# Transposing V and weight tiles in the loading DMA instead of on TensorE, in the backward pass of a two-layer decode kernel

## The chip, the cores and the metric

The kernel runs on one core of one Trainium2 chip. The metric is the device time of one execution, in microseconds. A few runs of the kernel before are repeated in each set, on the same chip as the kernels they are compared with. A ratio is the mean time of one kernel's fast runs over that of the other's of the same rounds, so it is not quite the ratio of the medians that stand beside it; its 95% interval is in brackets.

Engines in the profile: PE is TensorE (PEld its weight loads), DVE is VectorE, ACT is ScalarE, SP is SyncE, which issues the loads. SPq and ACTq are the two queues from which loads are issued here.

## The reference, cut to what matters

Forward and backward of two layers with one new token for each of two sequences. Attention runs over caches of 16384 positions, so each layer streams K and V (4 heads x 2 sequences x 16384 x 128, 32 MiB each), and the weights are used once per pass. The two layers share caches and weights.

```python
q = (x @ wq)...                                    # wq 1024 x 4096
scores = jnp.einsum("bhqd,bhkd->bhqk", q, k) * (Dh ** -0.5)
p = _softmax(scores); o = jnp.einsum("bhqk,bhkd->bhqd", p, v)
x = x + o.reshape(B, Sq, Hq * Dh) @ wo             # wo 4096 x 1024
h = _gelu(jnp.einsum("bsd,df->bsf", y, w1) + b1)   # w1 1024 x 3584
x = x + jnp.einsum("bsf,fd->bsd", h, w2) + b2
# ... two such layers, then jax.vjp: gradients of x, K, V and all weights
```

The backward products need the other orientation of what the forward pass used: dP = dO V^T needs V with its 128 columns on the partitions, and the products with w1, wo and wq of the backward pass need those weights transposed.

## The kernel before

Tiles are 128 partitions x 4096 bf16 (1 MiB; a w1 tile is 128 x 3584), in a pool of 7 load buffers. All loads are issued by SyncE. Where a transposed tile is needed, TensorE turns eight 128x128 blocks at a time into PSUM and VectorE or ScalarE copies them back to SBUF.

```python
def emit_T(cv, b, third):                       # V of the backward attention, K of the forward one
    tp = (px if third and tp_n["n"] % 3 == 0 else pt)([128, 8, 128], BF16, "tp")
    for j in range(8):
        PE.transpose(tp[:, j, :], cv[:, b * 8 + j, :], ident[:])
    kT = ktp.tile([128, 8, 128], BF16, name="kT", tag="kT")
    evac_bf16(kT[:]..., tp[:]..., 1024)         # VectorE or ScalarE, whichever has less to do
    return kT

class BwdPipe:                                  # w1 and wo of the backward products
    def push(self, wv, j, jj, o0, on):
        for o in range(on):
            PE.transpose(tp[:, o, :], wv[:, j, (o0 + o) * 128:(o0 + o + 1) * 128], ident[:])
        ...
    def pop(self):
        for o in range(on):
            PE.matmul(wide_out(self.out_ps, 2 * jj), lhsT=wT[:, o, :], rhs=wide_in(self.gT[:, o0 + o, :]), ...)

class Ahead:                                    # a weight turned in place ahead of its products: w2, wo of layer 0
    def row(self, j): ...; turn(w, ...)
    def products(self, j, out_ps, gT_bf): ...
# ...
# layer-1 backward attention: w2 rows join wq's rows in one list of side work, worked off between slots
                    wq_q.extend(n[2])                         # 8 transposes of wq rows
                if g == groups[-1] and c == 0 and b == 3:
                    for k in range(NLD - 2):
                        ahead.load(k)
                        wq_q.extend(lambda j=j: ahead.row(j) for j in range(j0, j0 + rb))
```

## Time and profile before

1181 us (1177.89 to 1181.94). The part that the change touches lies between the end of the layer-1 forward pass (459.5 us) and the start of the last stage (761.6 us):

| stretch of the kernel before | us |
|---|---|
| w1 and wo backward, layer 1 | 52.6 |
| layer-1 backward attention with wq, and the w2 tail | 190.7 |
| w2 product, then w1 and wo backward, layer 0 | 58.8 |
| last stage (layer-0 backward attention and all gradient stores) | 421.2 |

The page of the kernel before: first busy time per engine, then the span in 40 slices (busy share of the DMA engines in tenths, and what they moved).

```profile
span 1182.8 us, 40678 instructions
PE 981.7 (83%) x17981; PEld 754.3 (64%) x17981; DVE 606.4 (51%) x1264; ACT 538.2 (46%) x1366; POOL 63.9 (5%) x113
DMA  9999999998999989989999939767999999999996
GB/s 370 416 417 417 417 417 395 393 341 365 417 417 413 412 312 416 393 327 414 411 396 383 365 136 398 293 231 296 372 403 420 420 413 418 419 421 418 423 423 267
```

PE at 83% looks like the bound, but the DMA row is full almost everywhere, at 417 GB/s in many slices (423 at most). Averages over the span settle nothing; the stretches do. The windows view of the kernel before, for the four stretches of the table: length, then busy us (and count) of PE, PEld, DVE, ACT, POOL, then the granted TensorE clock, the DMA share and GB/s.

```profile
459.50:512.10 52.60, 43.95 (x965) 42.50 (x965) 28.09 (x74) 17.96 (x32) 0.00 (x0) 0.92 1.03 399
512.10:702.80 190.70, 169.41 (x3589) 144.74 (x3590) 72.56 (x158) 67.08 (x118) 0.00 (x0) 0.95 0.89 349
702.80:761.60 58.80, 51.56 (x1201) 48.50 (x1198) 27.59 (x70) 19.15 (x34) 0.71 (x1) 0.94 0.90 341
761.60:1182.80 421.20, 363.90 (x4749) 217.95 (x4748) 305.33 (x532) 282.62 (x541) 57.86 (x98) 0.75 0.94 380
```

In the first stretch the DMA is full. In the second and third both PE and DMA are at about 90%: two limits that nearly balance. The groups of instructions that the change removes, in the kernel before between 459 and 772 us (count, busy us, mean ns, idle before them):

```profile
L379 PE MATMUL tp<-ident,kv_V 128*128 128x128 bf16 x864 | 69.9, 227 | 7.7 <-DMA kv_V<-in_A_v_cache_dram 6.3 <-issue 0.6 <-DVE kT L151 0.2
L263 PE MATMUL wtp<-ident,wt 128*128 128x128 bf16 x704 | 56.9, 228 | 2.5 <-DMA wt<-in_B_w_dram 1.3 <-issue 1.2
L313 PE MATMUL wtq<-ident,wqt 128*128 128x128 bf16 x256 | 20.3, 224 | 2.0 <-DMA wqt<-in_A_wq_dram 1.8
```

Matmuls are pipelined: a mean of 227 ns is not what one costs. The timeline of PE in the kernel before (start, us, what) gives the true cost. Eight transposes start 0.45 us before the products that follow them, so about 56 ns each; and there is no gap at all.

```profile
745.07 0.61 PE L313 MATMUL turn<-ident,wt 128*128 128x128 bf16 x8
745.52 0.35 PE L340 MATMUL wob_b<-gA_all,wt 128*128 128x32 bf16 x8
745.72 0.61 PE L313 MATMUL turn<-ident,wt 128*128 128x128 bf16 x8
```

Two views of the loads. The DMA part of the page says in how many packets they moved, and how many of these were small; the timeline of SyncE's queue shows that issuing a 1 MiB load takes it 0.33 us.

```profile
DMA packets 89133, 449.35 MB, mean 380 GB/s; under 512 B 7026, under 2 KB 7026, under 8 KB 49788
593.85 0.33 SPq L368 DMA_DIRECT2D kv_V<-in_A_v_cache_dram  x1
594.59 0.33 SPq L368 DMA_DIRECT2D kv_K<-in_A_k_cache_dram  x1
```

### The profile page before, as it was taken

Reading aid. Unit: us, or ns where it says so; the run is one execution under the profiler, and the core shown is the slowest. Engines: PE = TensorE matmul, PEld = TensorE weight load, DVE = VectorE, ACT = ScalarE, POOL = GpSimd, SP = SyncE. Lnnn points to the kernel's source line nnn. Section 1 sums busy time; section 2 is a strip of 40 time slices with the busy share of each in tenths; the row PEclk is TensorE's granted clock in tenths of the full one; section 3 lists DMA queues with packets and bytes.
Section 4 is the critical chain, followed back from the end, with each engine's and each line's share of the span. In section 5 each row is a group of like instructions: output and inputs, shape, how many; then the busy total and the mean of one; then the engine's idle time right before and its main releaser. Section 6 shows DMA issues by size and latency. Waiting matters only on the chain. (4 is left out here: it accounts for less than half of the span.)

```text
span 1182.8 us, 40678 instructions
## 1 busy us (share of the span) xinstructions
PE 981.7 (83%) x17981; PEld 754.3 (64%) x17981; DVE 606.4 (51%) x1264; ACT 538.2 (46%) x1366; POOL 63.9 (5%) x113
## 2 busy tenths in 40 slices
PE   4989795488879876899798988888988889999885
PEld 3867673488767756887676788755555554555552
DVE  1544351233535423444243334567877877786774
ACT  0544341022535421334233323366766867685773
POOL 0000000000000000000000000001111111111111
PEclk9988886597989876989998998987877877786785
DMA  9999999998999989989999939767999999999996
GB/s 370 416 417 417 417 417 395 393 341 365 417 417 413 412 312 416 393 327 414 411 396 383 365 136 398 293 231 296 372 403 420 420 413 418 419 421 418 423 423 267
DMA packets 89133, 449.35 MB, mean 380 GB/s; under 512 B 7026, under 2 KB 7026, under 8 KB 49788
## 3 DMA queue, kind: packets, MB, share of 16 engines
q1 hardware_dynamic: 72204, 348.17, 73.9%
q0 software_dynamic: 16752, 98.59, 20.3%
q8 instruction: 140, 2.29, 0.8%
q14 instruction: 37, 0.30, 0.1%
HBM read 348.14 MB, written 98.58 MB: 378 GB/s over the span
## 5 line engine op out<-in xcount | busy, mean ns | idle before, releaser
L148 ACT COPY kT<-tp 128x512 int32<-128x512 int32 x181 | 106.3, 587 | 266.0 <-PE tp L379 258.2
L151 DVE COPY kT<-tp 128x1024 bf16<-128x1024 bf16 x187 | 128.1, 691 | 152.7 <-PE tp L379 143.1
L379 PE MATMUL tp<-ident,kv_K 128*128 128x128 bf16 x1728 | 144.7, 233 | 4.6 <-DMA kv_K<-in_A_k_cache_dram 4.0
L379 PEld LDWEIGHTS <-kv_K 128*128 128x128 bf16 x1728 | 109.9, 104 | 5.2 <-DMA kv_K<-in_A_k_cache_dram 5.1
L159 DVE CAST big<-xm 128x512 bf16<-128x512 f32 (+1 forms) x140 | 91.0, 685 | 30.3 <-PE xm L1100 15.9
L156 ACT CAST big<-xm 128x512 bf16<-128x512 f32 (+1 forms) x157 | 85.7, 593 | 25.1 <-PE xm L959 15.1
L521 PEld LDWEIGHTS <-kT 128*128 128x128 bf16 x2048 | 76.7, 98 | 28.7 <-issue 22.9
L521 PE MATMUL sc<-qT_bf,kT 128*128 128x8 bf16 x2048 | 92.2, 171 | 0.7 <-issue 0.7
L263 PE MATMUL wtp<-ident,wt 128*128 128x128 bf16 x928 | 77.0, 231 | 3.6 <-issue 2.3
L297 PEld LDWEIGHTS <-wt 128*128 128x128 bf16 x1696 | 49.1, 103 | 46.4 <-issue 15.3
L485 ACT ACTIVATE e_all<-sc,negm 128x64 bf16<-128x64 f32 x256 | 77.1, 343 | 1.3 <-DVE negm L480 1.1
L379 PE MATMUL tp<-ident,kv_V 128*128 128x128 bf16 x864 | 69.9, 227 | 7.7 <-DMA kv_V<-in_A_v_cache_dram 6.3
L159 DVE CAST keepK<-xm 128x512 bf16<-128x512 f32 x95 | 61.7, 684 | 18.8 <-PE xm L1100 13.6
L405 PE MATMUL acc_all<-kv_V,e_all 128*16 128x256 bf16 x864 | 46.5, 295 | 29.2 <-DMA kv_V<-in_A_v_cache_dram 16.2
L148 ACT COPY wT<-wtp 128x512 int32<-128x512 int32 (+1 forms) x60 | 34.5, 576 | 78.2 <-PE wtp L263 63.4
L151 DVE COPY wT<-wtp 128x1024 bf16<-128x1024 bf16 (+1 forms) x64 | 40.5, 636 | 52.0 <-PE wtp L263 48.7
L156 ACT CAST keepK<-xm 128x512 bf16<-128x512 f32 x102 | 54.8, 592 | 19.7 <-PE xm L1100 18.9
L263 PEld LDWEIGHTS <-wt 128*128 128x128 bf16 x928 | 58.9, 103 | 4.4 <-issue 2.9
L379 PEld LDWEIGHTS <-kv_V 128*128 128x128 bf16 x864 | 54.6, 102 | 9.8 <-DMA kv_V<-in_A_v_cache_dram 7.3
L159 DVE CAST keepV<-xm 128x512 bf16<-128x512 f32 (+1 forms) x78 | 50.8, 685 | 18.8 <-PE xm L1100 14.8
L156 ACT CAST keepV<-xm 128x512 bf16<-128x512 f32 (+1 forms) x94 | 51.0, 594 | 19.8 <-PE xm L1100 16.8
L485 ACT ACTIVATION_READ_ACCUMULATOR e_all<-sc,negm 128x1 f32 x256 | 59.8, 234 | 0.0
(325 smaller groups left out, 1762.7 us busy)
## 6 DMA issues: line engine op xcount, KB each, us to landing
kv_K<-in_A_k_cache_dram SPq DMA_DIRECT2D x81, 1024.0 KB, 12.9
kv_V<-in_A_v_cache_dram SPq DMA_DIRECT2D x81, 1024.0 KB, 11.9
out_dram<-big POOLq DMA_DIRECT2D x36, 1024.0 KB, 17.0
wt<-in_A_wo_dram SPq DMA_DIRECT2D x32, 1024.0 KB, 11.1
wt<-in_B_w_dram SPq DMA_DIRECT2D x32, 896.0 KB, 14.4
out_dram<-keepK POOLq DMA_DIRECT2D x22, 1024.0 KB, 17.3
out_dram<-keepV POOLq DMA_DIRECT2D x18, 1024.0 KB, 17.2
wt<-in_A_wq_dram SPq DMA_DIRECT2D x16, 1024.0 KB, 9.1
```

The lines of the kernel that those rows point to most:

```text
L148: S.copy(out=dst.bitcast(I32), in_=src.bitcast(I32))
L151: V.tensor_copy(out=dst, in_=src)
L156: S.copy(out=dst, in_=src)
L159: V.tensor_copy(out=dst, in_=src)
L263: PE.transpose(tp[:, o, :], wv[:, j, (o0 + o) * 128:(o0 + o + 1) * 128], ident[:])
L297: PE.matmul(fps[:, jo, :].rearrange("p (a b) -> p a b", b=2), lhsT=wv[:, j, jo * 128:(jo + 1) * 128], rhs=xT_bf[:, j0 + j, :].unsqueeze(1) ...
L379: PE.transpose(tp[:, j, :], cv[:, b * 8 + j, :], ident[:])
L405: PE.matmul(self.acc[cg:cg + 16, :], lhsT=coef(u), rhs=self.cv[:, t:t + 2, :].rearrange("p t d -> p (t d)"), start=False, stop=True, tile_ ...
L485: S.activation(out=e_all[:, g, f * half:(f + 1) * half, l, h, :], in_=sc[g][f][:, h, :].rearrange("p (a b) -> p a b", b=2), func=ACT.Exp, ...
L521: PE.matmul(sc[g][f][:, :, t % TH], lhsT=kT[:, j, :], rhs=q_bf[:, g, :], start=True, stop=True)
```

## The change

The intent is to take these transposes off TensorE, and their copies off VectorE and ScalarE, by letting the DMA crossbar transpose while it loads. 67 loads become transposing ones: 27 of V, 8 of wq, 16 of wo, 16 of w1, 65 MiB in all (27 + 8 + 16 + 14). K, w2, and everything in the forward pass and the last stage stay as they were, but for one kept V tile (tile XG below), which is turned in place in layer 1 and then used turned in the last stage.

```diff
+    def w_load_T(W, j0, rb, c0, n_cols):
+        wt = ld.tile([128, LDW], BF16, name="wtT", tag="ld")
+        wv = wt[:, 0:rb * n_cols].rearrange("p (o r) -> p o r", r=rb * 128)
+        nc.sync.dma_start_transpose(wv, W[j0 * 128:(j0 + rb) * 128, c0:c0 + n_cols])
+        return wv
+    def products_T(wv, j, jj, out_ps, gT):
+        for o in range(JO):
+            PE.matmul(wide_out(out_ps, 2 * jj), lhsT=wv[:, o, j * 128:(j + 1) * 128], rhs=wide_in(gT[:, o, :]), ...)
+    def v_load_T(g, c):
+        t = ld.tile([128, LDW], BF16, name="kv_VT", tag="ld")
+        tv = t[:].rearrange("p (t d) -> p t d", d=128)
+        nc.sync.dma_start_transpose(tv, Vv[g, :, c * TC:(c + 1) * TC, :].rearrange("p t d -> p (t d)"))
+        return tv
# ... layer-1 backward attention
-                        cv = kv_load("V", g, c)
-                    kTs[s] = emit_T(cv, b, True)
-                    if s % 7 == 3 and v_turns:
+                        cv = held_tiles["V"][:]... if (g, c) == (XG, 0) else v_load_T(g, c)
+                    kTs[s] = cv[:, b * 8:(b + 1) * 8, :]
+                    if s % 5 == 3 and v_turns:
# ... w1 and wo of layer 1 (and, likewise, both of layer 0, where wo had been turned ahead)
-        _, dmps = w_pass(B_w1, D, F, "dm_ps", gT_bf=dh_all[:, :, lsl(l)])
+        dmps = w_bwd(B_w1, D, F, "dm_ps", dh_all[:, :, lsl(l)])
-        _, dops = w_pass(A_wo, HD, D, "do_ps", gT_bf=gA_all[:, :, lsl(l)])
+        dops = w_bwd(A_wo, HD, D, "do_ps", gA_all[:, :, lsl(l)])
# ... wq: loaded transposed; its list of transposing steps is now empty
+                box[j] = w_load_T(A_wq, j, 4, kv * D, D)
+        turns = [lambda j=j: turn_row(j) for j in range(DJ)] if get_ is not None else []
# ...
```

More of the change, by code (lines that the diff above doesn't have):

```diff
@@ L251, in w_load, with w_bwd @@
         return wv
+    def w_load_T(W, j0, rb, c0, n_cols):
[4 more added lines that the diff above has]
+    def products_T(wv, j, jj, out_ps, gT):
+        JO = wv.shape[1]
+        for o in range(JO):
+            PE.matmul(wide_out(out_ps, 2 * jj), lhsT=wv[:, o, j * 128:(j + 1) * 128], rhs=wide_in(gT[:, o, :]),
+                      start=(o == 0), stop=(o == JO - 1))
+    def w_bwd(W, n_in, n_out, name, gT):
+        ps = px([128, 512], F32, name)
+        for j0, rb in w_chunks(n_in, n_out):
+            wv = w_load_T(W, j0, rb, 0, n_out)
+            for j in range(rb):
+                products_T(wv, j, j0 + j, ps, gT)
+        return pairs(ps, n_in // 128)
     class BwdPipe:
@@ L589, in attn_bwd @@
         last_q = []
-        v_turns = deque(lambda c=c, b=b: turn(held_tiles["V%d" % c][:, b * 1024:(b + 1) * 1024],
+        v_turns = deque(lambda w=w, b=b: turn(held_tiles[w][:, b * 1024:(b + 1) * 1024],
                                               lambda: pt([128, 8, 128], BF16, "turn"))
-                        for c in range(NCH) for b in range(NB))
+                        for w in ["V"] + ["V%d" % c for c in range(NCH)] for b in range(NB))
         while s < len(slots) + 2 or sch.busy():
@@ L600, in attn_bwd @@
                     if b == 0:
-                        cv = kv_load("V", g, c)
-                    kTs[s] = emit_T(cv, b, True)
-                    if s % 7 == 3 and v_turns:
+                        cv = held_tiles["V"][:].rearrange("p (t d) -> p t d", d=128) if (g, c) == (XG, 0) else \
+                            v_load_T(g, c)
+                    kTs[s] = cv[:, b * 8:(b + 1) * 8, :]
+                    if s % 5 == 3 and v_turns:
                         v_turns.popleft()()
@@ L779, in load @@
         def load(j):
-            wt = ld.tile([128, LDW], BF16, name="wqt", tag="ld") if get_ is None else get_("wq", kv, j)
-            box[j] = wt[:].rearrange("p (j n) -> p j n", j=4)
             if get_ is None:
-                nc.sync.dma_start(box[j], wq_v[:, j:j + 4, kv * D:(kv + 1) * D])
+                box[j] = w_load_T(A_wq, j, 4, kv * D, D)
+            else:
+                box[j] = get_("wq", kv, j)[:].rearrange("p (j n) -> p j n", j=4)
         def turn_row(j):
@@ L790, in products @@
             for j in range(DJ):
+                if get_ is None:
+                    products_T(box[j - j % 4], j % 4, j, ps, dq_all[:, hs, 2 * l:2 * l + 2])
+                    continue
                 for o in range(8):
@@ L800, in dq_in @@
                 V.tensor_copy(out=dq_all[:, hs, 2 * l + b], in_=dqT[:, b * HKV + kv, :])
-        return [lambda j=j: load(j) for j in (0, 4)], dq_in, [lambda j=j: turn_row(j) for j in range(DJ)], products
+        turns = [lambda j=j: turn_row(j) for j in range(DJ)] if get_ is not None else []
+        return [lambda j=j: load(j) for j in (0, 4)], dq_in, turns, products
     def attn_in_bwd(l, gT, dn, hook=lambda: None):
@@ L851 @@
     sv = saved["m0"]
-    _, dmps = w_pass(B_w1, D, F, "dm_ps", gT_bf=dh_all[:, :, lsl(0)])
-    wob = Ahead(A_wo, HD, "wob")
-    for k in range(len(wob.chunks)):
-        wob.load(k)
-    rest = deque(lambda j=j: wob.row(j) for j in range(wob.J - 4))
+    dmps = w_bwd(B_w1, D, F, "dm_ps", dh_all[:, :, lsl(0)])
     dm = wrk.tile([128, DJ, 2], F32, name="dm_sb")
     V.tensor_copy(out=dm[:], in_=dmps[:])
-    dn = ln_bwd(dm[:], sv["y2"][:], sv["rstd2"][:], "dn", lambda: some(rest, 4))
-    dx = ln_bwd(dn[:], sv["y1"][:], sv["rstd1"][:], "dx", lambda: some(rest, 4))
+    dn = ln_bwd(dm[:], sv["y2"][:], sv["rstd2"][:], "dn")
+    dx = ln_bwd(dn[:], sv["y1"][:], sv["rstd1"][:], "dx")
     g1 = vec.tile([128, DJ, 2], F32, name="gM0")
@@ L863 @@
     V.tensor_copy(out=gA_all[:, :, lsl(0)], in_=g1[:])
-    dops = px([128, 512], F32, "wob_b")
-    for j in range(wob.J + 4):
-        some(rest, 1)
-        if j >= wob.J - 4 and j < wob.J:
-            wob.row(j)
-        if j >= 4:
-            wob.products(j - 4, dops, gA_all[:, :, lsl(0)])
+    dops = w_bwd(A_wo, HD, D, "wob_b", gA_all[:, :, lsl(0)])
     TP = [pt([128, 8, 128], BF16, "tpm%d" % i) for i in range(2)]
@@ L873 @@
         V.memset(t[:].bitcast(F32), 0.0)
-    do_delta(0, pairs(dops, HQ))
+    do_delta(0, dops)
     rowsA = ld.tile([128, LDW], BF16, name="rowsA", tag="ld")
@@ L1175, in score0 @@
             return
+        if (g, c) == (XG, 0):
+            done("V", g, c)
         if c == 0:
@@ L1241 @@
                 cv = get("V", *chunks[i])[:].rearrange("p (t d) -> p t d", d=128)
-                kT = ktp.tile([128, 8, 128], BF16, name="kT", tag="kT")
-                tp = mtp()
-                for j in range(8):
-                    PE.transpose(tp[:, j, :], cv[:, b * 8 + j, :], ident[:])
-                evac_bf16(kT[:].rearrange("p a b -> p (a b)"), tp[:].rearrange("p a b -> p (a b)"), 1024)
-                kTs[s] = kT
-                if b == NB - 1:
-                    done("V", *chunks[i])
+                if chunks[i] == (XG, 0):
+                    kTs[s] = cv[:, b * 8:(b + 1) * 8, :]
+                else:
+                    kT = ktp.tile([128, 8, 128], BF16, name="kT", tag="kT")
+                    tp = mtp()
+                    for j in range(8):
+                        PE.transpose(tp[:, j, :], cv[:, b * 8 + j, :], ident[:])
+                    evac_bf16(kT[:].rearrange("p a b -> p (a b)"), tp[:].rearrange("p a b -> p (a b)"), 1024)
+                    kTs[s] = kT
+                    if b == NB - 1:
+                        done("V", *chunks[i])
             if 0 <= s - 2 < NS:
```

## The prediction

> **What bounds the kernel now.** Most of the span is bound by loads: in the busy-time table by 30 us windows the 16 DMA engines are at 0.97 to 1.0 and move up to 417 GB/s. The changed part runs from 460 to 772 us, by the timeline:
> - w1 and wo of layer 1 (460-512): DMA 1.03, 400 GB/s, TensorE 44 of 52 us.
> - layer-1 backward attention (512-690): DMA 0.92, 362 GB/s; TensorE 159 of 178 us. TensorE is the limit at the start (DMA 0.5 in the first 12 us, and the load queue waits for transposes) and at the end (w2 rows); between them DMA stands at 416 GB/s.
> - w2 tail (690-712): TensorE and a serial chain; all seven load buffers hold w2, DMA 0.61.
> - w1 and wo of layer 0 (712-772): TensorE 51 of 60 us; DMA 1.03, then 0.75.
>
> **What the change removes.** From the groups by line: about 864 transposes of V, 224 of w1 twice, 256 of wo twice, 256 of wq. Eight take about 0.44 us in sequence in the timeline (55 ns each), so about 110 us of TensorE's sequence, and with it about 230 evacuations of 0.6 to 0.7 us on VectorE and ScalarE. It adds only four turns of a kept V tile, which later disappear from the last stage.
>
> **What it adds.** No bytes; but 65 MiB (27 V, 8 wq, 16 wo, 14 w1; 68 MB) go through the crossbar. At 417 GB/s they would take 163 us. The whole result hangs on the rate. The Trainium skill disagrees with itself: "Advanced Engine Details and Errata", section "X-Bar Transpose (TRN2)", calls transposing DMAs as fast as regular ones, while "DMA: Bandwidth & Descriptors", section "Latency and other measured facts", gives 261 GB/s measured with a non-contiguous middle dimension and 350-400 contiguous. The trace before has no such DMA, so it decides nothing.
>
> **Estimate per stage** (from these rates and the bytes above; plain loads at 417):
> - At 417: attention -12 us (its TensorE-bound start and end), w2 tail -4, w1/wo of layer 0 -13 (DMA 15.7 MB in 38 us plus a chain): 1152 us.
> - At 350: attention 0, layer-1 w1/wo +7, layer-0 w1/wo -6: about 1181.
> - At 300: +16, +15, 0: about 1212.
> - At 261: +35, +22, +8: about 1246.
>
> TensorE relief is off the path wherever DMA is full, so a slower transfer is paid nearly in full. I expect a rate near 300. Forward stages and the last stage (772 to the end) should stay equal within a few us.
>
> **Prediction: 1208 us, range 1148 to 1285.** Faster by over 2%: 0.22; within 2%: 0.30; slower: 0.48.
>
> **What would show each step.** TensorE busy falls by some 200 us (busy counts pipelined spans), VectorE and ScalarE by some 70 each. In the DMA issues, transposing loads land later than the plain ones, and 1 MB of them takes over 3 us of full queue rather than 2.5. In the windows of attention, DMA share is 1.0 but GB/s falls to 320-360, and what TensorE waits for there becomes the DMA of V and w, not evacuations. Span of attention 185-215 us instead of 178. If attention shrinks below 170 us at over 400 GB/s, the crossbar is free and I am wrong.
>
> **What would make it wrong.** A crossbar at full rate (faster by 2-3%); one far slower, or one that holds up the plain loads queued behind it on the same queue (over 1285 us); the wait for w1 in layer 0 (its loads start only when w2's buffers are freed) being exposed at the slower rate.

## The result, and the profile after

1302.88 us median (1301.82 to 1306.54) against 1181.46 us: ratio 1.104 [1.1009, 1.1072]. The kernel is slower by 121 us, outside the predicted range. The page of the changed kernel, in the same rows as before:

```profile
span 1301.7 us, 35939 instructions
PE 882.3 (68%) x15869; PEld 642.3 (49%) x15869; DVE 524.3 (40%) x1136; ACT 455.7 (35%) x1222; POOL 63.7 (5%) x113
DMA  9999999989999999999999993998899999999996
GB/s 373 416 417 417 417 406 393 368 346 417 418 416 403 339 200 235 257 271 282 266 298 260 294 289 99 215 235 313 356 382 391 420 418 417 424 421 414 421 423 254
```

TensorE lost 99 us of busy time, VectorE and ScalarE 82 each. From slice 15 to 27 the DMA is as full as before but for one slice (the w2 tail), and yet moves only 200 to 300 GB/s. The windows of the changed kernel, for the same four stretches:

```profile
457.90:530.00 72.10, 16.89 (x486) 15.23 (x485) 7.36 (x41) 0.25 (x1) 0.00 (x0) 0.50 1.11 219
530.00:805.80 275.80, 126.78 (x2468) 92.23 (x2469) 31.36 (x97) 22.14 (x40) 0.00 (x0) 0.57 1.02 262
805.80:881.60 75.80, 23.87 (x718) 21.45 (x717) 8.38 (x39) 0.00 (x0) 0.71 (x1) 0.57 1.07 218
881.60:1301.70 420.10, 364.18 (x4717) 215.48 (x4717) 304.35 (x530) 282.34 (x539) 57.70 (x98) 0.74 0.96 390
```

The stretches grew by 19.5, 85.1 and 17.0 us, and the last stage is as it was. In the first and third, where almost nothing but transposing loads moves, the rate is 219 and 218 GB/s. The granted clock of TensorE falls to 0.50 and 0.57 there; the engine is busy for 16.9 of 72.1 and 23.9 of 75.8 us, and mostly waits for data in the rest. The groups of the changed kernel that now wait:

```profile
L609 PE MATMUL dp<-doT_bf,kv_VT 128*128 128x8 bf16 x864 | 33.9, 176 | 11.5 <-DMA kv_VT<-in_A_v_cache_dram 11.5
L432 PE MATMUL acc_all<-kv_K,dX 128*16 128x256 bf16 x432 | 31.6, 389 | 117.1 <-DMA kv_K<-in_A_k_cache_dram 116.3 <-DVE acc_all L420 0.8
L263 PE MATMUL dm_ps<-dh_all,wtT 128*128 128x32 bf16 x448 | 14.8, 188 | 51.3 <-DMA wtT<-in_B_w_dram 46.7 <-DVE dh_all L754 4.6
```

116 us are waits for K, which is loaded as before: it stands in the queue behind V. Blaming the K loads here would be a misreading; the V load in front is what became longer. The timeline of PE over the products with wo of layer 0, which were without a gap before:

```profile
866.11 1.04 PE L263 MATMUL wob_b<-gA_all,wtT 128*128 128x32 bf16 x32 [3.38 <-DMA wtT<-in_A_wo_dram]
870.67 1.03 PE L263 MATMUL wob_b<-gA_all,wtT 128*128 128x32 bf16 x32 [3.52 <-DMA wtT<-in_A_wo_dram]
876.15 1.03 PE L263 MATMUL wob_b<-gA_all,wtT 128*128 128x32 bf16 x32 [4.45 <-DMA wtT<-in_A_wo_dram]
```

Finally the loads of the changed kernel: the packets, the transposing issues (the last number is us from issue to landing), and the timeline of SyncE's queue, where a line merges consecutive issues of one kind.

```profile
DMA packets 338632, 449.05 MB, mean 345 GB/s; under 512 B 274338, under 2 KB 274338, under 8 KB 302764
kv_VT<-in_A_v_cache_dram SPq DMA_TRANSPOSE x27, 8.8
wtT<-in_A_wo_dram SPq DMA_TRANSPOSE x16, 6.9
526.07 13.05 SPq L397 DMA_TRANSPOSE kv_VT<-in_A_v_cache_dram  x3
806.86 34.89 SPq L257 DMA_TRANSPOSE wtT<-in_B_w_dram  x8
841.85 35.62 SPq L257 DMA_TRANSPOSE wtT<-in_A_wo_dram  x8
```

The queue needs 13.05 / 3 = 4.35 us for a V tile, 4.45 us for a wo tile and 4.36 us for the smaller w1 tile, which is 241, 236 and 210 GB/s. A plain 1 MiB load at 417 GB/s takes 2.5 us. The number of packets under 512 bytes rose from 7026 to 274338. A packet is one piece of a load, moved by one DMA engine. The trace's records of single packets say how big they are and how long each took (medians; not a view of the profile, counted from the trace):

```
packet size      kernel before            changed kernel
     4 B         9 ns                     9 ns
   256 B         none                     266240 packets, 18 ns
  2048 B         86 ns                    85 ns
  4096 B         159 ns                   159 ns
  7168 B         275 ns                   275 ns
  8192 B         313 ns                   313 ns
```

266240 x 256 B is exactly 65 MiB: a transposing load moves in packets of 256 bytes. The kernel before already showed what such a packet should cost: its packets of 2048 and 8192 bytes give (313 - 86) / 6144 = 0.037 ns a byte, and so a fixed part of about 10 ns (its packets of 4 bytes take 9); 256 bytes should take about 20 ns, and 18 were measured.

The sum closes. From issue intervals, the extra load time is 27 x 1.84 us for V, 8 x about 2.1 for wq (from 9.20 us for two), 16 x 1.94 for wo, and 16 x 2.16 for w1: about 132 us. The loss is 121 us; against the same kernel with plain loads, which is the closer comparison and comes next, it is 133 us.

### The profile page after: what moved, and what is told of

It is laid out like the page before. It is cut to its first block, busy times and chain, and to the rows that moved or that the text cites. A ratio compares the mean times of both kernels' runs of the same rounds, so it can differ in the third digit from the quotient of the medians.

```text
span 1301.7 us, 35939 instructions
## 1 busy us (share of the span) xinstructions
PE 882.3 (68%) x15869; PEld 642.3 (49%) x15869; DVE 524.3 (40%) x1136; ACT 455.7 (35%) x1222; POOL 63.7 (5%) x113
## 5 line engine op out<-in xcount | busy, mean ns | idle before, releaser
L151 DVE COPY kT<-tp 128x1024 bf16<-128x1024 bf16 x145 | 99.1, 691 | 98.6 <-PE tp L406 91.5
L148 ACT COPY kT<-tp 128x512 int32<-128x512 int32 x111 | 65.2, 587 | 189.9 <-PE tp L406 184.7
L432 PE MATMUL acc_all<-kv_K,dX 128*16 128x256 bf16 x432 | 31.6, 389 | 117.1 <-DMA kv_K<-in_A_k_cache_dram 116.3
L156 ACT CAST big<-xm 128x512 bf16<-128x512 f32 x164 | 89.7, 593 | 29.0 <-PE xm L981 17.9
L159 DVE CAST big<-xm 128x512 bf16<-128x512 f32 x133 | 86.6, 686 | 26.4 <-PE xm L1122 14.4
L581 DVE TENSOR_TENSOR dX<-dp,e_all 128x256 bf16<-128x256 f32 x32 | 13.6, 424 | 194.4 <-PE dp L576 194.4
L263 PEld LDWEIGHTS <-wtT 128*128 128x128 bf16 x1216 | 35.9, 104 | 103.8 <-DMA wtT<-in_B_w_dram 51.3
L432 PEld LDWEIGHTS <-dX 128*16 128x16 bf16 x960 | 14.9, 86 | 136.2 <-issue 132.1
L318 PEld LDWEIGHTS <-wt 128*128 128x128 bf16 x1696 | 48.9, 104 | 45.9 <-issue 14.7
L432 PE MATMUL acc_all<-kv_V,e_all 128*16 128x256 bf16 x864 | 46.5, 295 | 28.3 <-DMA kv_V<-in_A_v_cache_dram 15.8
L981 PE MATMUL xm<-rowsA,rowsB 4*128 4x512 bf16 x120 | 46.1, 458 | 8.6 <-ACT big L156 1.6
## 6 DMA issues: line engine op xcount, KB each, us to landing
out_dram<-big POOLq DMA_DIRECT2D x36, 1024.0 KB, 15.8
```

The lines of the kernel that those rows point to most:

```text
L148: S.copy(out=dst.bitcast(I32), in_=src.bitcast(I32))
L151: V.tensor_copy(out=dst, in_=src)
L156: S.copy(out=dst, in_=src)
L159: V.tensor_copy(out=dst, in_=src)
L263: PE.matmul(wide_out(out_ps, 2 * jj), lhsT=wv[:, o, j * 128:(j + 1) * 128], rhs=wide_in(gT[:, o, :]), start=(o == 0), stop=(o == JO - 1))
L318: PE.matmul(fps[:, jo, :].rearrange("p (a b) -> p a b", b=2), lhsT=wv[:, j, jo * 128:(jo + 1) * 128], rhs=xT_bf[:, j0 + j, :].unsqueeze(1) ...
```

## The experiments

The theories, named as in the expectations. P: the DMA engines spend time on each 256-byte packet, crossbar (the part that transposes during a load) or not. X: the crossbar itself is slow. S: issuing a transposing load is what takes long (SyncE stands 4.35 us at each in the timeline above, against 0.33 us for a plain one). R: the restructuring costs, since wo is no longer turned ahead and buffers are held differently.

### The same kernel with plain loads

```diff
-        nc.sync.dma_start_transpose(wv, W[j0 * 128:(j0 + rb) * 128, c0:c0 + n_cols])
+        nc.sync.dma_start(wt[:, 0:rb * n_cols].rearrange("p (j n) -> p j n", j=rb),
+                          W[j0 * 128:(j0 + rb) * 128, c0:c0 + n_cols].rearrange("(j p) n -> p j n", p=128))
-        nc.sync.dma_start_transpose(tv, Vv[g, :, c * TC:(c + 1) * TC, :].rearrange("p t d -> p (t d)"))
+        nc.sync.dma_start(tv, Vv[g, :, c * TC:(c + 1) * TC, :])
```

> The changed kernel with its 67 transposing loads replaced by plain loads of the same bytes into the same tiles at the same places; the values are wrong on purpose. Theory P (the engines pay for 256-byte packets), theory X (the crossbar itself is slow) and theory S (issuing a transpose is slow) all say that the whole loss lies in the loads: about 1150 to 1160 us, w1/wo stages and attention below those of the kernel before. Theory R (the loss comes from the restructuring: wo is no longer turned ahead, buffers are held longer) says it stays above 1181 us, near 1250 or more.

Measured: 1169.82 us (1166.76 to 1170.89), ratio 0.9904 [0.9868, 0.994]; the results are wrong. This is what the change would give if transposing while loading cost nothing. R falls: with plain loads the restructured kernel is no slower than the kernel before, so the loss comes with the transposing loads. But the gain is 11 us, not the 20 to 30 that was expected. The windows of this kernel (first three stretches):

```profile
460.60:500.60 40.00, 16.34 (x485) 14.92 (x485) 7.33 (x41) 0.25 (x1) 0.00 (x0) 0.50 1.03 400
500.60:700.70 200.10, 125.23 (x2470) 92.25 (x2471) 31.18 (x97) 22.15 (x40) 0.00 (x0) 0.60 0.90 356
700.70:748.30 47.60, 23.64 (x718) 21.42 (x717) 8.30 (x39) 0.00 (x0) 0.71 (x1) 0.61 0.97 368
```

The weight stretches are 12.6 and 11.2 us shorter than in the kernel before, and attention is 9.4 us longer. Most of the first and the last of these is bookkeeping. In the kernel before, loads ran ahead of TensorE, so its first stretch moved 399 GB/s x 52.6 us = 21.0 MB; here it moves 16.0 MB, and the other 5 MB, 12 us at 417 GB/s, fall into attention. The two stretches together went from 243.3 to 240.1 us. A wait at the end of attention is taken up again below.

This kernel and the changed one move nearly the same bytes in each stretch (16.0, 71.2 and 17.5 MB against 15.8, 72.3 and 16.5), so here the stretches can be compared: those of the changed kernel are 32.1, 75.7 and 28.2 us longer.

### Plain loads in runs of 256 bytes

```diff
-        nc.sync.dma_start_transpose(tv, Vv[g, :, c * TC:(c + 1) * TC, :].rearrange("p t d -> p (t d)"))
+        nc.sync.dma_start(tv, V256[g, :, c * TC:(c + 1) * TC, :])
+    V256 = A_v_cache.rearrange("b h (t p) d -> (b h) p t d", p=128)   # 256-byte rows dealt over the partitions
# ... and the weights likewise, as rows of 128 elements
```

> The same plain loads, but each 1 MB load is laid out so that it moves in runs of 256 bytes, without the crossbar; wrong values on purpose. Theory P: each packet takes 18 ns as in the changed kernel, 220 to 240 GB/s, and the kernel takes 1285 to 1320 us. Theory X: the packets go clearly faster without the crossbar (under 14 ns), and the time is below 1220 us. Theory S: no transposing instruction is issued, so about 1155 us.

Measured: 1314.08 us (1312.53 to 1316.41), ratio 1.1131 [1.1092, 1.117]; wrong results. There is no crossbar in it and no transposing instruction, and it is as slow as the changed kernel, even 11 us slower. (A run is a stretch of bytes that lies together in HBM.) The windows of this kernel:

```profile
458.00:531.50 73.50, 16.85 (x484) 15.19 (x484) 7.34 (x41) 0.25 (x1) 0.00 (x0) 0.50 1.14 216
531.50:814.40 282.90, 127.64 (x2468) 92.34 (x2469) 31.32 (x97) 22.15 (x40) 0.00 (x0) 0.57 0.96 254
814.40:894.80 80.40, 23.87 (x717) 21.60 (x717) 8.38 (x39) 0.00 (x0) 0.71 (x1) 0.57 1.09 212
```

Stretch for stretch these are nearly the rates of the changed kernel: 216, 254 and 212 GB/s against 219, 262 and 218. Runs of 256 bytes are enough for the whole loss, and X and S are not needed to explain it. What the crossbar would cost with longer runs is not shown: no run here transposes in anything but 256-byte packets. One detail differs from the expectation: only w1 moved in packets of 256 bytes (24 ns each at the median). V, wo and wq moved in packets of 1024 bytes (52224 of them, 51 MiB) that took 81 ns, so 20 ns for each run of 256 bytes, where the fit above would give 48 ns for a packet of 1024 bytes in one run. The cost goes with the runs, not with the packets. Theory P is right once "packet" is read as "run".

### Plain loads in runs of 512 bytes

The same edit with rows of 256 elements.

> Plain loads as in the kernel with 256-byte runs, but in runs of 512 bytes; wrong values on purpose. Theory P with a fixed part per run: the packets of the trace before (84 ns for 2048 bytes, 309 to 313 ns for 8192) give 9 ns plus 27 bytes per ns, so 28 ns for 512 bytes and 3.5 us for 1 MB, about 1.0 us more than the plain load; with 65 MB of them 1170 + 65 = 1225 to 1250 us, about half way back from 1314. If 256 bytes is a special case (a threshold), 512-byte runs cost next to nothing: below 1190.

Measured: 1230.8 us (1229.83 to 1232.63), ratio 1.0413 [1.0382, 1.0445]; wrong results. 61 us above the kernel with long runs, 83 us below the one with 256-byte runs. In the records, the 512-byte packets of w1 take 32 ns (expected 28), and packets of 2048 bytes in the first changed stretch (460 to 512 us), nearly all made of four runs, take 116 ns at the median, against 86 ns for 2048 bytes in one run. There is no threshold at 256 bytes: the cost per run is a fixed part and a part by bytes, and with short runs the fixed part weighs.

### K issued from ScalarE's queue

```diff
-            nc.sync.dma_start(t[:]..., src[g, :, c * TC:(c + 1) * TC, :])
+            kq["q"].dma_start(t[:]..., src[g, :, c * TC:(c + 1) * TC, :])   # nc.scalar in the layer-1 backward attention
```

> The changed kernel with the 27 K loads of the layer-1 backward attention issued from the queue of ScalarE instead of SyncE's, so that they need not stand behind a transposing load. Theories P and X: the engines are full either way, so 1303 us within 15. Theory S (SyncE's issue of a transpose is the limit and the engines have room): K flows beside V and about 27 x 2.5 = 68 us of attention go away, about 1240 us.

Measured: 1320.52 us (1315.22 to 1327.69), ratio 1.1169 [1.1117, 1.1221]; correct. The miss is a few us on the slow side of P's expectation; why K from a second queue is slower than behind V was not looked into. The 68 us that S expected did not come: K does not flow beside V for free, as the engines are full (DMA share 1.00 to 1.17 in the windows of its attention). The issues of this kernel, and a line of SyncE's timeline:

```profile
kv_K<-in_A_k_cache_dram ACTq DMA_DIRECT2D x27, 1024.0 KB, 7.5
kv_VT<-in_A_v_cache_dram SPq DMA_TRANSPOSE x27, 9.4
555.72 14.81 SPq L399 DMA_TRANSPOSE kv_VT<-in_A_v_cache_dram  x2
```

All 27 K loads came from the other queue, and V landed 9.4 us after issue instead of 8.8. The 4.35 us that SyncE stands at a transposing load are thus not what limits, and they are no fixed cost of issuing: with K on the other queue SyncE stands 14.81 / 2 = 7.4 us at a V load. That fits back pressure of full engines. The absence of a gain from the second queue (1320.5 against 1302.9 us) agrees with the Trainium skill, "DMA: Bandwidth & Descriptors", section "Issuing engines are not separate DMA queues": queues of different engines end on the same 16 DMA engines.

### The two halves of the change

V alone (weights as in the kernel before), and the weights alone (V by TensorE as before).

> The kernel before with only V of the layer-1 backward attention transposed by the loads (27 loads); weights as before. From 4.35 us for a transposing load against 2.5 us for a plain one, 27 x 1.85 = 50 us more loading, less a few us of TensorE relief at the start of attention: 1220 to 1235 us under P, X and S alike. If the mixing of plain and transposing loads cost much by itself, over 1250.

Measured: 1235.71 us (1233.12 to 1237.11), ratio 1.0463 [1.0427, 1.05]; correct. That is 0.7 us above the expected range.

> The other half of the change alone: w1, wo and wq of the backward products transposed by the loads (40 loads), V of the layer-1 backward attention by TensorE as in the kernel before. If the loss is simply added by each transposing load, this and the V-only kernel must add up to the change: 122 - 55 = 67 us over the kernel before, 1240 to 1255 us. If the parts overlap (one hides the other's cost), the two halves sum to clearly more than 122 us, this one over 1265.

Measured: 1247.8 us (1246.17 to 1250.09), ratio 1.0557 [1.0525, 1.0589]; correct. The halves lose 55 and 66 us, together 121, which is the loss of the whole. No half hides the other's cost: it is 55 / 27 = 2.0 us for each V load and 66 / 40 = 1.7 us for each load of a weight. These are net figures. V's is above the 1.84 us of the issue intervals, and in the timeline of the changed kernel a V load between K loads does take longer (three pairs of V and K in the 21.8 us from 539.84 to 561.64 us, so about 4.75 us for V beside 2.5 for K). That of the weights has TensorE's relief in it (11.2 us in the third stretch with plain loads), and also the wait at w2 of the next section, which the weights-only kernel has (15.0 us) and the V-only kernel has not (3.0 us); the two were not taken apart.

### What the emptied list cost

With plain loads TensorE waits 9.93 us at the first row of w2, and in the changed kernel 14.18 us (timelines of PE, first the kernel with plain loads, then the changed one):

```profile
661.85 0.40 PE L356 MATMUL w2b_f<-h_all,wt 128*128 128x32 bf16 x8 [9.93 <-DMA wt<-in_B_w_dram]
```

```profile
766.99 0.39 PE L355 MATMUL w2b_f<-h_all,wt 128*128 128x32 bf16 x8 [14.18 <-DMA wt<-in_B_w_dram]
```

The w2 rows stand in a list behind wq's eight transposes. The change empties those eight entries, so the first w2 row moves forward in TensorE's order, ahead of attention work whose data is already there, and blocks it until its load has landed. The edit puts eight empty entries in their place:

```diff
-                    wq_q.extend(n[2])
+                    wq_q.extend(n[2] or [lambda: None] * DJ)
```

> The kernel with plain loads instead of transposing ones (1170 us), and 8 empty entries put where the removed wq transposes stood in TensorE's list of side work, so that the first row of w2 again comes as late as in the kernel before; wrong values on purpose. In the trace of 1170 us TensorE waits 9.9 us at that row for a load of w2, with attention work standing behind it in its order. If this order is what ate the gain of attention, 5 to 10 us come back: 1160 to 1165 us. If the end of attention is bound by the w2 rows and their buffers wherever they stand, it stays at 1168 to 1172.

Measured: 1158.09 us (1156.95 to 1161.38), ratio 0.9802 [0.9786, 0.9819]; wrong results. That is 2 us better than the expected range.

> The same 8 empty entries in the changed kernel, where TensorE waits 14.2 us at the first row of w2: 1290 to 1298 us if the order matters, 1300 to 1306 if not. Either way the bulk of the loss, over 100 us, must stay, as it lies in the rate of the loads.

Measured: 1294.97 us (1291.93 to 1295.19), ratio 1.0956 [1.0936, 1.0976]; correct. So the emptied list cost about 12 us with plain loads and 8 to 10 us in the changed kernel (by medians and by ratios); the prediction had not seen it, but it is a small part of the loss. Where the time came back is clear only in the changed kernel: in its profiled executions attention with the w2 tail fell from 275.8 to 268.5 us. With plain loads it fell from 200.1 to 198.1 us only, and the rest of the difference lies in the last stage (420.7 to 416.3) and before the changed part (460.6 to 458.4), for which the order of the list is no explanation that was shown. As far as plain loads stand for it, 1158 us is what transposing loads at the full rate would have given with the order repaired.

### A mixture: only where the DMA has room

In the kernel before, TensorE works without a gap through the products with wo of layer 0, while SyncE's loads of wo are issued by 747 us. There, transposing loads could be free. The eight loads in the timeline of SyncE's queue:

```profile
719.26 27.71 SPq L250 DMA_DIRECT2D wt<-in_A_wo_dram  x8
```

```diff
-    for k in range(len(wob.chunks)):
+    NT = 4                                     # 2 in the other variant
+    for k in range(len(wob.chunks) - NT):
         wob.load(k)
+    for j0, rb in wob.chunks[-NT:]:
+        woT[j0] = w_load_T(A_wo, j0, rb, 0, D)
# ... products of these rows from the transposed tiles, with no turn
```

> The kernel before, with only the last 2 of the 8 loads of wo of layer 0 transposed by the DMA. In that stretch (714 to 761 us) TensorE works without a break and the DMA queue has room at its end, so 2 x 1.8 us of transposes leave the path and 2 x 1.9 us of load time fall where the queue was idle: 2 to 4 us faster than the kernel before (ratio 0.997 to 0.998). If any transposing load is paid in full wherever it stands: 4 us slower (1.003).

Measured: 1180.19 us (1178.33 to 1182.63), ratio 0.9985 [0.996, 1.0011]; correct. The interval holds 1, so a gain is not shown; it does leave out the 1.003 of full payment.

> The same with the last 4 of 8 loads of wo transposed by the DMA: TensorE's part falls by 7 us, the loads take 7.6 us longer and end at about 757 us, so 3 to 5 us faster than the kernel before (ratio 0.996 to 0.9975), no longer limited by TensorE. If transposing loads are paid in full: 8 us slower (1.006).

Measured: 1179.32 us (1175.52 to 1181.08), ratio 0.997 [0.9941, 0.9998]; correct. This is the fastest correct version here, by about 0.3%, and its interval barely leaves 1 out. The window of its third stretch:

```profile
703.80:759.80 56.00, 43.69 (x1073) 40.96 (x1070) 22.28 (x62) 14.45 (x26) 0.71 (x1) 0.92 1.06 308
```

56.0 us against 58.8, TensorE busy 43.7 against 51.6, DMA share 1.06 against 0.90: four transposing loads filled the room in the queue, and there is none left. A loss of 8 us, which full payment would have meant, is excluded by the interval.

## Why the prediction was wrong

- **The step that failed is the rate**: "I expect a rate near 300". It measured 210 to 241 GB/s. Even the slow end of the estimate, "At 261: +35, +22, +8: about 1246", assumed more than the chip gave, and the range ended at 1285. The cause is the run length: 256 bytes at 18 ns instead of 8192 at 313 ns. In the prediction's own sum (an estimate from its text and the runs): at 300 GB/s the 68 MB take 64 us more than at 417, and it took 33 us of relief off that to reach 1212 us. The runs show 133 us more (changed kernel against plain loads) and 11 us of relief (plain loads against the kernel before). So of the 91 us between 1212 and 1303, the rate made 69 and relief that did not come 22.
- "The trace before has no such DMA, so it decides nothing" was wrong too. The packet records before give a fixed part of 10 ns and 0.037 ns a byte, which puts a 256-byte packet at about 20 ns; a 1 MiB tile is 4096 of them, 256 for each of the 16 engines, so 5.1 us for 1 MiB if packets did not overlap (an estimate; 4.35 us was measured, and the DMA share of 1.1 in the windows shows that they do overlap a little). A hint at the 256 bytes was to be had from the Trainium skill, "DMA: Bandwidth & Descriptors", section "SDMA does more than copy", which calls the operation a "256B-tile transpose"; that each 256 bytes move as a packet of their own, only the trace of the changed kernel shows.
- **Right**: "a slower transfer is paid nearly in full" where the DMA is full. The two halves add up to the whole, and about 132 us of extra load time (by issue intervals) became 133 us against the same kernel with plain loads.
- **Near in the total, partly by luck**: the full-rate case, 1152 us. Plain loads with the order repaired gave 1158. By stretch, layer 0's w1 and wo fit (58.8 to 46.4 us, -12 against -13), but layer 1's weights and attention with the w2 tail together gave -5 (243.3 to 238.3) where -16 was foretold, and -5 came in the last stage, where nothing was. And the change as written would have given only 1170, as its side-work list let a w2 row block attention; the prediction had no term for this (8 to 10 us of the 121).
- **Wrong in part, by stretch**: the signs said attention 185 to 215 us with 320 to 360 GB/s, so 207 to 237 us with the 22 us of the w2 tail; with the tail it was 276 us (191 before) at 262 GB/s. The waits moved to the DMA as foretold, but mostly to K's loads behind V's, not V's. That transposing loads land later was wrong: V landed after 8.8 us, wo after 6.9 and w1 after 7.2 (plain ones in the kernel before, over its whole span: 11.9, 11.1 and 14.4).
- **Wrong in size**: TensorE's busy time fell by 99 us, not some 200. The groups that went away sum to about 166 us (69.9 + 56.9 + 20.3, and 19 for the 256 turns of wo of layer 0), and what stayed got longer where the granted clock was lower, 0.50 to 0.57 (the products with K from a mean of 281 to 389 ns; that the clock is the reason was not tested). VectorE and ScalarE fell by 82 each (foretold some 70).
- **Right**: forward stages and the last stage are unchanged (421.2 and 420.1 us).

## What to carry to other kernels

Before moving a transpose into a load, find the run length in which the transposing load moves, and price it with the packet times that the trace already holds: a fixed part per run plus a part per byte. Where the DMA is full, TensorE's transposes are free and the load's are not; only in a stretch with an idle queue and a TensorE without gaps was any gain seen here (0.3%, barely clear of noise), and only as many loads can gain as fit the idle time. When stretches of two kernels are compared, compare their bytes too: loads that run ahead move time from one stretch to the next. And when work is deleted from a list that also sets the order of other work, look at what moves forward into its place.

## What the Trainium skill lacked or had wrong

- "Advanced Engine Details and Errata", section "X-Bar Transpose (TRN2)", says transposing DMAs are as fast as regular ones, with 350-400 GB/s expected. Here they moved 210 to 241 GB/s beside 417 for plain loads, with source rows of 2 to 8 KB contiguous.
- "DMA: Bandwidth & Descriptors", section "Latency and other measured facts", gives 261 GB/s for a non-contiguous middle dimension and 350-400 for the contiguous case. No case here reached either; V, whose source rows are 8 KB contiguous, had 241.
- The same page, section "Why small descriptors are slow (HBM only)", counts 3 cycles on top of 8 for a 256-byte descriptor, 27%, besides 32 bytes of descriptor. Here the fixed part is about as large as the rest: 18 ns for 256 bytes where the slope of long packets gives 9.5, and plain loads in 256-byte runs of 1 MiB tiles lost as much as transposing ones (1314 and 1303 us).
- The same section says that joining consecutive descriptors into a packet amortizes the per-packet cycles. If the profile's packets are what it means, little came of it here: 1024-byte packets of four runs took 81 ns, about 20 ns a run, and in the kernel with 256-byte runs wo in such packets moved 214 GB/s (855 to 880 us) beside 203 for w1 in packets of one run (815 to 845 us).
- No page explains why w1's transposing loads (128 rows of 7168 bytes) moved 210 GB/s and wo's 236; the runs here leave this open.
